# A Transformer block on one core: more buffers for keys, features and values, feature sums taken whole, and another written order

## The chip, the cores and the metric

The kernel runs on one core of a Trainium2 chip. A core has five engines with instruction queues of their own: TensorE (PE, matmuls), VectorE (DVE), ScalarE (ACT), GpSimd (POOL) and SyncE (SP, which here only issues DMAs). Every queue runs in order, and an instruction that depends on another engine waits for its semaphore. The metric is the device time of one execution in microseconds (us); lower is better.

## What is computed

For x of shape 2048 x 448 in bf16, the block is a linear attention with softmax feature maps, followed by a gated MLP, both on a layer-normalized input and both added back:

```python
def _A_ref(x, wqkv, w_phi, wo):                      # 16 heads of 28
    qkv = (x @ wqkv).reshape(B, S, 3, H, Dh) ...     # q, k, v
    pq = jnp.einsum("bhsd,hdf->bhsf", q, w_phi); pk = jnp.einsum("bhsd,hdf->bhsf", k, w_phi)
    phi_q = concat([softmax(pq), softmax(-pq)]); phi_k = concat([softmax(pk), softmax(-pk)])
    kv = jnp.einsum("bhsf,bhsd->bhfd", phi_k, v); z = jnp.einsum("bhsf->bhf", phi_k)
    num = jnp.einsum("bhqf,bhfd->bhqd", phi_q, kv)
    den = jnp.einsum("bhqf,bhf->bhq", phi_q, z)[..., None] + 1e-6
    return (num / den) ... @ wo
def _B_ref(x, w_gate, w_up, w_down):                 # F = 1792
    return (sigmoid(x @ w_gate) * (x @ w_up)) @ w_down
h = x + _A_ref(_layernorm(x), ...); h2 = h + _B_ref(_layernorm(h), ...)
```

## The kernel before

The 2048 rows are 16 tiles of 128 rows, numbered t; two neighbouring tiles are a pair, pr. All weights and all of x stay in SBUF.

**Start.** x and the weights are loaded. The feature weights are folded into the key and query weights on TensorE (kT, WkT, wM, W2: lines 535 to 575), so that keys come out of one matmul as feature logits. 14 matmuls on a zero tile (fill, line 988) run while the weights load.

**K/V stage, tile by tile.** bst and agg (lines 583, 585) are the layernorm's statistics on VectorE; ve and rstd (586, 588) give the reciprocal deviation, the power on GpSimd; xn (602 on ScalarE, 603 on VectorE) normalizes a tile into one of NXP buffers. Tiles 0 to 3 are transposed on TensorE (xP, xT), the others two at a time by a DMA transpose that SyncE issues (xT, line 621). pa and pb (line 637) are the two halves of a tile's matmuls: seven pairs that run side by side in the two row halves of the array, one for the key logits, one for v. ScalarE takes exp(l) and exp(-l) into ek (ekp 657, ekm 659), one of NEK buffers. v is copied out of PSUM into v1 (one of NV buffers) on ScalarE or VectorE; the copy and most PSUM evictions have the helper's line 425.

Each of the 32 softmaxes of a row (16 heads, two signs) needs its sum over 28 features. In the kernel before, sa (line 667) adds the two halves of the 28 pairwise into an f32 tile half_s, on GpSimd (12 tiles) or VectorE (4 tiles), and ss (673, VectorE) reduces the rest. rs (682) is the reciprocal, and phi (684) multiplies ek by it, 896 elements per partition, into one of NPHI buffers: all 16 on VectorE. kv (696) accumulates phi-transpose times v over the tiles in one PSUM bank; after tile 15, kvz (751, VectorE) takes the sums out.

**Attention stage.** q (line 736) are eight groups of matmuls, (gp, c) for two head groups and four chunks of 512 rows, with exponentials eqp and eqm on ScalarE. They need no kvz and stand between the K/V matmuls as well. num (772) are the numerators of one tile, ocp takes them out of PSUM (ScalarE or VectorE, line 425); rSm, rr, b, c, rd and o (788 to 800, VectorE) combine and divide; pair 0 is transposed on TensorE (oP, oT), the others by DMA (od, oT); wo (833) is the output projection; bst2, agg2, ve2, rstd2, hn (867 to 877) normalize h again; hP/hT transpose it.

**MLP.** Chunks of 2, 4, 4, 4 and 2 tiles. ga and gu (line 934) are the gate and up matmuls of one of 14 slices; sig (943, ScalarE) takes a tanh, hh (951, VectorE) multiplies; dn (968) is the down projection, fin (975) adds it to x, st (978) stores. The attention of the later pairs runs between the gate and up matmuls.

**The order is written out.** Every piece of work is a task with a name, an engine, a cost that only a planner uses, and the tasks that it depends on. With the text ORDER non-empty, no planner runs: `stored` (line 129) reads the order of all tasks from it, and `emit` (250) gives each task to its engine's queue in that order, with the waits that the dependencies need:

```python
for v in table.split():
    t = self.tasks[names[int(v) // 32]]
    t.eng = t.engs[int(v) % 4]
    ...
        t.got, gate = t.banks[int(v) // 4 % 8]
```

So each number holds the task (in order of creation, times 32), the PSUM banks (times 4) and which of the task's possible engines runs it.

Of the kernel before, what the change touches and what calls it, by code (L numbers as in the profile page):

```python
# [5 lines left out]
dt = mybir.dt  # L6
ALU = mybir.AluOpType
# [3 lines left out]
P = 128  # L11
D = 448
# [20 lines left out]
NFILL = 14  # L33
# [288 lines left out]
def build(nc, A_x, A_wqkv, A_w_phi, A_wo, B_w_gate, B_w_up, B_w_down, out):  # L322
# [13 lines left out]
    out_t = out[0].rearrange("(n p) d -> p n d", p=P)  # L336
    wd_v = B_w_down.rearrange("(ft p) n -> p ft n", p=P)

    NXP, NEK, NPHI, NV, NOP, NO, NHP, NSG, NSA = 8, 4, 3, 4, 3, 2, 2, 4, 2
    SPLIT = range(NT)  # L340

    with ExitStack() as es:
# [686 lines left out]
```

## Time and profile before

| | |
|---|---|
| time, median of 3 runs | 208.22 us (207.96 to 210.22) |
| the profiled execution | 207.67 us, of which its span is 205.9 us |
| TensorE busy | 197.2 us (96%) |
| VectorE busy | 135.6 us (66%) |
| ScalarE busy | 96.5 us (47%) |
| GpSimd busy | 30.6 us (15%) |
| granted TensorE clock | 1.00 |

The span runs from the first to the last instruction that the profiler recorded. Shares are averages over stages with different limits, so a stage has to be read by itself. A row of the lists of groups names the line, the engine, the operation, what it writes and reads with the shape, the count, the busy time with the mean duration in ns, and the idle time before it with what ended it. A timeline row has the start, the time from the first to the last end of the merged instructions, and the idle time in brackets. Two instructions in a row on VectorE overlap a little at their ends, so the spacing of their starts is shorter than their duration.

### The profile page before, as it was taken

Reading aid. Unit: us, or ns where it says so; the run is one execution under the profiler, and the core shown is the slowest. Engines: PE = TensorE matmul, PEld = TensorE weight load, DVE = VectorE, ACT = ScalarE, POOL = GpSimd, SP = SyncE. Lnnn points to the kernel's source line nnn. Section 1 sums busy time; section 2 is a strip of 40 time slices with the busy share of each in tenths; the row PEclk is TensorE's granted clock in tenths of the full one; section 3 lists DMA queues with packets and bytes.
Section 4 is the critical chain, followed back from the end, with each engine's and each line's share of the span. In section 5 each row is a group of like instructions: output and inputs, shape, how many; then the busy total and the mean of one; then the engine's idle time right before and its main releaser. Section 6 shows DMA issues by size and latency. Waiting matters only on the chain.

```text
span 205.9 us, 5431 instructions
## 1 busy us (share of the span) xinstructions
PE 197.2 (96%) x2278; PEld 107.1 (52%) x2278; DVE 135.6 (66%) x312; ACT 96.5 (47%) x172; POOL 30.6 (15%) x56
## 2 busy tenths in 40 slices
PE   7899998998988999999999999999999999999993
PEld 2544555455445876554444444544444455796553
DVE  2999999997998996789823875435446415351241
ACT  2579999799998773443311333003334400442000
POOL 3738653420003110001100001100001000000000
PEclk9999999999999999999999999999999999999999
DMA  5996477764022493700450000620000031000034
GB/s 167 279 277 128 76 188 200 181 223 142 3 57 48 73 173 81 197 3 3 94 111 3 0 0 3 124 51 0 3 0 5 2 79 20 0 3 0 25 111 156
DMA packets 35109, 16.94 MB, mean 82 GB/s; under 512 B 26828, under 2 KB 34060, under 8 KB 35084
## 3 DMA queue, kind: packets, MB, share of 16 engines
q1 hardware_dynamic: 34140, 15.78, 33.1%
q10 hardware_dynamic: 944, 0.80, 1.4%
q8 instruction: 18, 0.29, 0.6%
q14 instruction: 7, 0.06, 0.1%
HBM read 8.98 MB, written 1.84 MB: 53 GB/s over the span
## 4 chain that ended last, share of the span: by engine, by line
PE 78%; DVE 12%; ACT 4%; DMA 2%; issue 1%; POOL 1%
PE bank L934 42%; PE bank L968 21%; PE bank L637 5%; PE bank L833 4%; PE bank L736 3%; DMA x_sb<-in_A_x_dram 2%; DVE phi L684 2%; PE bank L696 1%; DVE ssum L673 1%; DVE xn_pad L603 1%; DVE st L583 1%; ACT xn_pad L602 1%; ACT ek L659 1%; DVE b_sb L792 1%; DVE b_sb L795 1%
## 5 line engine op out<-in xcount | busy, mean ns | idle before, releaser
L934 PE MATMUL bank<-xnT,wg_sb 64*128 64x512 bf16 (+1 forms) x490 | 87.4, 333 | 0.1
L934 PE MATMUL bank<-xnT,wu_sb 64*128 64x512 bf16 (+1 forms) x490 | 87.4, 333 | 0.0
L943 ACT ACTIVATE sg_sb<-bank 128x512 f32<-128x512 f32 (+1 forms) x70 | 34.6, 513 | 77.9 <-PE bank L934 74.0
L951 DVE SCALAR_TENSOR_TENSOR hh<-sg_sb,bank 128x512 bf16<-128x512 f32 (+1 forms) x70 | 39.1, 576 | 28.4 <-ACT sg_sb L943 28.1
L934 PEld LDWEIGHTS bank<-xnT,wg_sb 64*128 64x128 bf16 x490 | 45.3, 94 | 21.9 <-issue 1.9
L934 PEld LDWEIGHTS bank<-xnT,wu_sb 64*128 64x128 bf16 x490 | 45.1, 94 | 15.5
L968 PE MATMUL bank<-wd_sb,hh 128*128 128x448 bf16 (+1 forms) x238 | 43.1, 342 | 0.0
L968 PEld LDWEIGHTS bank<-wd_sb,hh 128*128 128x128 bf16 x238 | 22.9, 98 | 20.1 <-issue 1.4
L975 DVE SCALAR_TENSOR_TENSOR x_sb<-bank,x_sb 128x448 bf16<-128x448 f32 (+1 forms) x17 | 9.9, 594 | 28.3 <-PE bank L968 28.3
L637 PE MATMUL bank<-Wk,xnT 64*128 64x448 bf16 x112 | 22.1, 350 | 0.4 <-ACT Wq L425 0.3
L637 PE MATMUL bank<-Wv,xnT 64*128 64x448 bf16 x112 | 21.6, 350 | 0.0
L746 ACT ACTIVATE eq<-bank 128x1024 bf16<-128x1024 f32 x16 | 16.3, 1067 | 0.7 <-PE bank L736 0.6
L871 POOL TENSOR_SCALAR rs<-mv 128x2 f32<-128x2 f32 x5 | 1.3, 256 | 99.6 <-DVE mv L869 50.3
L667 POOL TENSOR_TENSOR half_s<-ek 128x448 f32<-128x448 bf16 x12 | 12.9, 1078 | 15.3 <-ACT ek L657 7.0
L425 ACT CAST opm<-bank 128x960 bf16<-128x960 f32 x14 | 13.7, 1014 | 2.8 <-PE bank L772 2.1
L833 PE MATMUL bank<-wo_sb,oT 64*128 64x448 bf16 x112 | 13.3, 350 | 0.9 <-DVE oT L425 0.6
L736 PE MATMUL bank<-xnT,Wq 64*128 64x512 bf16 x112 | 14.0, 377 | 0.1
L637 PEld LDWEIGHTS bank<-Wk,xnT 64*128 64x128 bf16 x112 | 9.1, 94 | 6.9 <-PE bank L637 1.0
L637 PEld LDWEIGHTS bank<-Wv,xnT 64*128 64x128 bf16 x112 | 9.2, 94 | 4.3
L684 DVE TENSOR_TENSOR phi<-ek,rsum 128x896 bf16<-128x896 bf16 x16 | 10.3, 655 | 0.3 <-PE bank L696 0.2
L583 DVE BATCH_NORM_STATS2 st<-x_sb 128x6 f32<-128x448 bf16 x16 | 9.4, 612 | 1.7 <-DMA x_sb<-in_A_x_dram 1.7
L657 ACT ACTIVATE ek<-bank 128x448 bf16<-128x448 f32 x16 | 9.7, 630 | 1.3 <-PE bank L637 1.3
(91 smaller groups left out, 185.4 us busy)
## 6 DMA issues: line engine op xcount, KB each, us to landing
wg_sb<-in_B_w_gate_dram SPq DMA_DIRECT2D x4, 448.0 KB, 3.8
wu_sb<-in_B_w_up_dram SPq DMA_DIRECT2D x4, 448.0 KB, 3.7
out_dram<-x_sb SPq DMA_DIRECT2D x15, 112.0 KB, 1.8
wd_sb<-in_B_w_down_dram SPq DMA_DIRECT2D x7, 224.0 KB, 2.7
x_sb<-in_A_x_dram SPq DMA_DIRECT2D x2, 448.0 KB, 5.8
wq_raw<-in_A_wqkv_dram SPq DMA_DIRECT2D x4, 128.0 KB, 5.3
x_sb<-in_A_x_dram SPq DMA_DIRECT2D x2, 224.0 KB, 4.5
x_sb<-in_A_x_dram ACTq DMA_DIRECT2D x2, 224.0 KB, 4.9
```

The source lines that it names most:

```text
L425: return e.copy(dst, src) if hasattr(e, "activation") else e.tensor_copy(dst, src)
L583: task(("bst", t), "dve", dve(D), lambda e, t=t: e.bn_stats(st1[:, t % 4, :], X(t)), [x_ld[t], opt(("agg", t - 4))])
L637: r = e.matmul(bank[bk][:, 0:D], lhsT=half(xnT, hi)[:, t, k, :], rhs=half(w, hi)[:, k, :], start=(i == 0), stop=(i == 6), tile_position=(6 ...
L667: task(("sa", t), None, 0.88, lambda e, t=t, s=s: e.tensor_tensor(half_s[:, t % NSA].rearrange("p (a n) -> p a n", a=4 * G), ek[:, s].rear ...
L684: task(("phi", t), None, 1.68, lambda e, t=t, s=s: e.tensor_tensor(phi[:, t % NPHI, :, :, 0:DH, :].rearrange("p a g d h -> p (a g) d h"), ...
L736: r = e.matmul(bank[bb[j]], lhsT=half(Wq2, hi)[:, k, 2 * g:2 * g + 2].rearrange("p c d h -> p (c d h)"), rhs=half(xnT, hi)[:, 4 * c:4 * c ...
L746: task((key, gp, c), "act", act_p(1024), lambda e, gp=gp, c=c, sg=sg, nm=nm: e.activation(eq[c][:, sg, 2 * gp:2 * gp + 2, :], wide[got(nm) ...
L833: r = e.matmul(bank[bb[j]][:, 0:D], lhsT=half(oT, hi)[:, pr % NO, j, k, :], rhs=half(wo_sb, hi)[:, k, :], start=(i == 0 and not res), stop ...
L934: r = e.matmul(bank[b][:, 0:N], lhsT=half(w, hi)[:, k, fs], rhs=half(hnT, hi)[:, t0:t0 + n, k, :], start=(i == 0), stop=(i == 6), tile_pos ...
L943: task(("sig", f_, c), "act", act_p(N), lambda e, j=j, N=N, nm=nm: e.activation(sg_sb[:, j % NSG, 0:N], bank[got(nm)[0]][:, 0:N], ACT.Tanh ...
L951: task(("hh", f_, c), "dve", dve(N), lambda e, j=j, N=N, nm=nm, f_=f_, c=c: e.scalar_tensor_tensor(hhT[c % 2][:, f_, 0:N], sg_sb[:, j % NS ...
L968: r = e.matmul(bank[b][:, c0:c1], lhsT=hhT[c % 2][:, f_, o:o + P], rhs=wd_sb[:, f_, c0:c1], start=(f_ == 0), stop=(f_ == FT - 1))
```

## The change

Five things change. (1) The buffers of xn go from 8 to 10, ek from 4 to 6, phi from 3 to 6, v1 from 4 to 6, and opm (what ocp writes) from 3 to 4 pairs. (2) SPLIT is empty: the 16 sa tasks and half_s go, and ss reduces all 28 features of each softmax from ek. (3) Ten of the 16 phi run on GpSimd: tiles 0, 1, 2, 4, 6, 7, 10, 11, 12 and 14. (4) 12 fill matmuls stand in place of 14. (5) ORDER is another table. Two dependencies are stated more exactly (which transposes free an xn or an o_pad buffer), and xn asks for its engine by the task, not by the engine object.

```diff
-NFILL = 14
+NFILL = 12
...
-    NXP, NEK, NPHI, NV, NOP, NO, NHP, NSG, NSA = 8, 4, 3, 4, 3, 2, 2, 4, 2
-    SPLIT = range(NT)
+    NXP, NEK, NPHI, NV, NOP, NO, NHP, NSG, NSA = 10, 6, 6, 6, 4, 2, 2, 4, 2
+    SPLIT = ()
...
-        half_s = sb("half_s", [P, NSA, D], dt.float32)
+        half_s = sb("half_s", [P, NSA, D], dt.float32) if len(SPLIT) else None
...
-                free = opt(("xT", (t - NXP) // 2 * 2)) or opt(("xT", t - NXP))
+                free = opt(("xT", t - NXP if t - NXP in PE_X else (t - NXP) // 2 * 2))
...
-                    if hasattr(e, "activation"):
+                    if K.tasks[("xn", t)].eng == "act":
...
-                fac(rden[:, s2], DH), ALU.mult), [("rd", pr), opt(("oT", pr - NO))])
+                fac(rden[:, s2], DH), ALU.mult), [("rd", pr), opt(("oT", pr - NO)), opt(("oT", pr - NO, 0)), opt(("oT", pr - NO, 1))])
```

The form of ss that then runs was in the kernel already, for tiles not in SPLIT:

```python
task(("ss", t), "dve", dve(896), lambda e, s=s: e.tensor_reduce(
    ssum[:, s, :].rearrange("p (a h) -> p a h", h=2),
    ek[:, s].rearrange("p a (g d h) -> p (a g) h d", g=2 * G, h=2), AX.X, ALU.add),
```

Read out of the two tables, the queues around the change are these (name and tile; one line break has no meaning).

VectorE before, from the first statistics to kvz:

```
bst0 agg0 ve0 bst1 agg1 xn0 bst3 bst2 agg3 agg2 xn1 bst7 bst6 xT1 bst5 xn2 xn3 xT0 bst4 agg5 agg6 agg4 agg7 ve4
bst9 bst10 bst8 nm4 xn4 xn5 agg9 agg10 agg8 bst11 agg11 ss0 rs0 v1.0 ve8 phi0 ss1 bst13 bst15 xn8 bst14 rs1 agg15
agg13 bst12 ss2 phi1 rs2 ss3 agg14 agg12 rs3 ve12 phi2 phi3 mm12 v1.5 ss4 ss5 rs4 rs5 phi4 sa6 phi5 xn13 ss6 rs6
ss7 rs7 phi6 phi7 ss8 rs8 phi8 xn14 v1.10 ss9 sa10 ss10 rs9 rs10 phi9 sa12 ss11 phi10 ss12 rs11 phi11 rs12 ss13
phi12 rs13 sa15 phi13 ss15 rs15 ss14 phi15 rs14 phi14 kvz
```

VectorE after:

```
bst0 bst1 agg0 agg1 ve0 ve1 bst3 agg3 bst2 xn0 xn1 bst5 agg2 bst4 ve2 bst6 agg5 bst7 agg6 agg4 agg7 xn2 ve4 xn3 mm4
xT2 nm4 xn4 xn5 bst10 xn6 bst8 bst9 bst11 agg10 agg8 agg11 agg9 ss1 ss0 rs0 xn9 rs1 bst14 bst15 bst13 ss2 agg13 rs2
bst12 ss3 agg12 agg14 agg15 xn10 rs3 ss4 ss5 xn13 rs4 xn12 ss7 rs7 rs5 phi3 phi5 xn14 xn15 ss6 ss8 rs6 rs8 ss9 ss11
phi8 rs9 rs11 ss10 ss12 rs10 phi9 v1.13 rs12 ss13 ss14 rs13 rs14 phi13 ss15 rs15 phi15 kvz
```

VectorE behind kvz, to the first normalized h: before `ocp1 ocp3 rSm0 rr0 b0 rSm1 c0 rr1 b1 rd0 c1 o0 rd1 rSm2 o1 rr2 od1 oT0 oT0 b2 c2 rd2 o2 od2 bst2 ... b3 c3 hn1 hn0`, after `ocp0 rSm0 rr0 ocp3 b0 rSm1 c0 rSm2 rr1 rr2 rd0 b1 o0 c1 rSm3 rd1 b2 oT0 o1 od1 c2 rd2 rr3 o2 b3 od2 bst2.0 bst2.1 agg2 agg2 hc0 ve2 ocp8 hn1 hn0`.

GpSimd after: `... rstd8 nm8 phi0 phi1 phi2 ve12 mm12 rstd12 nm12 phi4 phi7 phi6 phi11 phi10 phi12 phi14`, then the later reciprocal deviations.

TensorE after, from the first V matmuls: `va0 wM wM vb0 xP2 xP3 pa0 pb0 pa3 pb3 pa2 pb2 wM wM wM pa5 pa4 pb5 pa6 pb4 pb6 pa7 wM kv0 kv1 pb7 qa0.0 kv2 q0.0 pa9 pa8 pb9 pb8 pa11 kv3 kv4 kv5 pb11 pa10 pa12 pb10 qa1.0 pb12 q1.0 kv6 kv7 kv8 pa13 pa14 pb13 pb14 pa15 qa1.1 pb15 q1.1 qa0.1 kv9 q0.1 kv10 kv11 kv12 kv13 kv14 kv15 qa0.3 num0 ...`.

SyncE's loads: before `x0 wk1 wph x4 wq0 wq3 x8 wq2 wv0 wv1 wq1 x12` with wk0, x2 and x6 on ScalarE's queue; after `x0 wk1 wk0 x4 wph x6 wv1 wv0 wo wq3 wq2 wq1 wq0 x8 x12` with x2 alone on ScalarE's.

93 rows, old and new, of the table ORDER are left out of this document.

## The prediction

> **What bounds the kernel now.** I read the busy time by stretches first, cutting the span at TensorE's first K/V matmul (11.76 us), at the first read of the feature sums (49.38) and at the first gate/up matmul (66.45). Columns: busy us of each engine with its instructions, clock, DMA.
>
> ```profile
> core 0: us, PE busy (x) PEld busy (x) DVE busy (x) ACT busy (x) POOL busy (x), PEclk, DMA share, GB/s
> 0.00:11.76 11.76, 9.74 (x66) 4.99 (x66) 7.58 (x21) 5.29 (x10) 5.76 (x22) 1.00 0.92 236
> 11.76:49.38 37.62, 36.64 (x568) 18.81 (x567) 35.51 (x87) 34.67 (x66) 17.36 (x21) 1.00 0.73 181
> 49.38:66.45 17.07, 14.65 (x300) 7.92 (x299) 15.75 (x38) 16.18 (x21) 1.62 (x2) 1.00 0.17 33
> 66.45:205.90 139.45, 136.19 (x1354) 75.32 (x1350) 76.73 (x168) 40.38 (x78) 5.82 (x11) 1.00 0.22 49
> ```
>
> In the last stretch TensorE idles 3.26 us, nearly all of it behind its last matmul. The MLP is matmul after matmul, and nothing in the change touches its work: whatever is won or lost is the time of the first gate/up matmul. In the K/V stretch TensorE idles only 0.98 us and in the next 2.42, so a better order can save about 3.4 us there. But VectorE is busy 35.51 of 37.62, and it ends the chain at both seams. The chain of waits (start, us, what), then VectorE's and TensorE's timelines (start, us; idle time before and who ended it in brackets):
>
> ```profile
> 42.90 0.86 PE bank L736 x8
> ...
> 48.64 0.75 PE bank L736 x6
> 49.39 0.41 PE bank L772 x16
> ...
> 63.75 0.42 DVE hn_pad L877
> 64.17 0.05 issue
> 64.22 0.72 PE bank L887 x8
> 64.94 0.86 PE bank L833 x8
> ...
> 202.75 0.39 DVE x_sb L975
> ```
>
> ```profile
> 7.79 1.03 DVE L603 TENSOR_SCALAR xn_pad<-x_sb,mv,rs 128x512 bf16<-128x512 bf16 x1
> ...
> 16.03 0.62 DVE L673 TENSOR_REDUCE ssum<-half_s 128x32 f32<-128x448 f32 x1
> ...
> 47.18 0.62 DVE L684 TENSOR_TENSOR phi<-ek,rsum 128x896 bf16<-128x896 bf16 x1
> 48.68 0.64 DVE L751 TENSOR_TENSOR kvz<-bank,dmask 128x464 bf16<-128x464 f32 x1 [0.88 <-PE bank L696]
> ...
> 55.41 0.61 DVE L800 TENSOR_TENSOR o_pad<-b_sb,rden 128x896 bf16<-128x896 bf16 x1
> ...
> 63.75 0.73 DVE L877 TENSOR_SCALAR hn_pad<-x_sb,mv,rs 128x512 bf16<-128x512 bf16 x2 [0.60 <-POOL rs L873]
> ```
>
> These are my anchors: first feature sum 16.03, last scaling done 47.80, kvz 48.68, first attention output 55.41, first normalized h 63.75.
>
> **The change, part by part.** The unit prices (groups by line and form: busy, mean ns) and the spacing of two operations in a row (timeline):
>
> ```profile
> L667 POOL TENSOR_TENSOR half_s<-ek 128x448 f32<-128x448 bf16 x12 | 12.9, 1078 | 15.3 <-ACT ek L657 7.0 <-ACT ek L659 3.7 <-DVE ssum L673 3.6
> L524 POOL TENSOR_TENSOR Wp<-wphd,maskW 112x224 bf16<-112x224 bf16 x2 | 1.1, 559 | 0.0
> L863 DVE TENSOR_TENSOR x_sb<-bank,x_sb 128x896 bf16<-128x896 f32 x7 | 7.6, 1086 | 0.4 <-PE bank L833 0.3
> L425 DVE CAST opm<-bank 128x960 bf16<-128x960 f32 x2 | 2.2, 1152 | 0.5 <-PE bank L772 0.5
> L425 DVE CAST v<-bank 128x448 bf16<-128x448 f32 x3 | 1.8, 603 | 0.3 <-PE bank L696 0.3
> L873 POOL TENSOR_TENSOR rs<-rs,neghalf 128x2 f32<-128x2 f32 x8 | 6.2, 770 | 5.8 <-DVE rs L871 5.4
> ```
>
> ```profile
> 6.51 1.15 DVE L583 BATCH_NORM_STATS2 st<-x_sb 128x6 f32<-128x448 bf16 x2
> 10.65 0.71 DVE L603 TENSOR_SCALAR xn_pad<-x_sb,mv,rs 128x512 bf16<-128x512 bf16 x2
> 23.67 1.15 DVE L684 TENSOR_TENSOR phi<-ek,rsum 128x896 bf16<-128x896 bf16 x2
> 25.74 1.14 DVE L673 TENSOR_REDUCE ssum<-half_s 128x32 f32<-128x448 f32 x2
> 26.80 0.55 DVE L682 RECIPROCAL rsum<-ssum 128x32 bf16<-128x32 f32 x2
> ```
>
> Two half sums take 1.14 us where one takes about 0.61, so the spacing is 0.53; likewise 0.53 for a scaling (phi), 0.54 for a bn_stats, 0.33 for a normalization (xn), 0.27 for a reciprocal (rs).
>
> *Full sums.* A reduction over 896 elements is not in the trace. The two casts from PSUM differ by 549 ns for 512 elements, 1.07 ns each; 448 more elements on top of 0.53 make a step of 1.00 us. The 896-element add of L863 took 1.086, the upper end; 0.53 would be the lower end, if the bf16 input were read twice as fast as the f32 one. I take 1.00, nearest to L863, which also has 896 elements. Sixteen add 16 x 0.47 = 7.5 us to VectorE.
>
> *Pairwise adds* go: four on VectorE (4 x 0.53 = 2.1), twelve on GpSimd (12.9 us).
>
> *Ten scalings to GpSimd.* VectorE loses 10 x 0.53 = 5.3. On GpSimd the two rows give 0.56 us for 224 elements and, undisturbed, 0.97 for 448 (row at 19.89 below: two in 1.90): by the line through both 1.79 for 896, by doubling 1.94. I take 1.8, since overhead doesn't double. GpSimd gets 18 us for 12.9, still far from full, but one scaling is 1.3 us slower than on VectorE.
>
> *Moved by the order:* four normalizations to VectorE (+1.3), two v evictions (about -1.1) and one xT copy (-0.3) off it, by the tables that follow from the order (section on the change). VectorE's sum for the stretch changes by 7.5 - 2.1 - 5.3 + 1.3 - 1.4 = 0.0 us. So the move buys no VectorE time; what counts is the waits. The normalizations leave ScalarE, which had slack of 3 us; that cover costs nothing. Two fewer fill matmuls lie in the start, before the weights have landed: nothing.
>
> *Loads.* Tiles 8 to 11 of x move from seventh place in SyncE's queue to twelfth, behind Wv, one wo piece and the wq pieces; the twelfth was tiles 12 to 15 (DMA queue's timeline, then the page's issues):
>
> ```profile
> 4.20 0.52 SPq L461 DMA_DIRECT2D x_sb<-in_A_x_dram  x1
> ...
> 8.54 0.56 SPq L461 DMA_DIRECT2D x_sb<-in_A_x_dram  x1
> ```
>
> ```profile
> x_sb<-in_A_x_dram SPq DMA_DIRECT2D x2, 448.0 KB, 5.8
> ```
>
> Issued near 8.5 with 5.8 to landing they are there by 14.3; their first bn_stats stands at about 14.2 in the sum below, so at most 0.1 shows, and without that cover each later us would delay VectorE's whole stretch. wk0 goes from ScalarE's queue to third on SyncE's, x6 to sixth; Wv comes earlier, which lets the first V matmuls start before K's. I cost these at nothing.
>
> *Waits.* VectorE and GpSimd exclude each other where both read SBUF in these forms:
>
> ```profile
> 28.81 1.06 DVE L603 TENSOR_SCALAR xn_pad<-x_sb,mv,rs 128x512 bf16<-128x512 bf16 x1
> 31.57 1.87 DVE L684 TENSOR_TENSOR phi<-ek,rsum 128x896 bf16<-128x896 bf16 x2
> ```
>
> ```profile
> 19.89 1.90 POOL L667 TENSOR_TENSOR half_s<-ek 128x448 f32<-128x448 bf16 x2 [0.44 <-ACT ek L657]
> 28.49 1.23 POOL L667 TENSOR_TENSOR half_s<-ek 128x448 f32<-128x448 bf16 x1 [1.52 <-ACT ek L657]
> 31.79 1.16 POOL L667 TENSOR_TENSOR half_s<-ek 128x448 f32<-128x448 bf16 x1 [0.28 <-ACT ek L659]
> ```
>
> The normalization at 28.81 took 1.06 instead of 0.41 and ended 0.15 us behind GpSimd's add (29.72). At 31.57 two scalings took 1.87 instead of 1.15: GpSimd's add, asked for in the first, ran between them. So a blocked operation waits for the whole of the other, and the one already waiting goes next. The Trainium skill, "SBUF — State Buffer", section "Who interferes with whom", says this too: a VectorE instruction with two SBUF inputs contends with a GpSimd instruction that reads SBUF, and the second to issue fully blocks. It speaks against this change, since the blocker grows from 0.97 to 1.8 us; these rows agree. Without it the waits below would be nil (first rival).
>
> Now VectorE's new queue, added up. xn1 ends at about 8.7, as before (8.82). Six batches of statistics and two normalizations bring it to 12.4; xT2 waits for tile 2's transposes, which stand behind the first V matmuls on TensorE, until 13.0; then xT2, nm4, xn4, xn5, xn6, four bn_stats and four aggregations: the first sum starts at **17.15, 1.1 later** than 16.03. From there to phi15: 16 sums 16.0, 16 reciprocals 4.3, 6 scalings 3.2, 6 normalizations 2.0, 4 bn_stats and 4 aggregations 2.6, one v 0.5: 28.6 us. Before, the same count gives 28.9 of 31.8, so 2.9 were waits. New waits, from placing GpSimd's scalings behind their reciprocals: xn10 behind phi2 0.25; phi3 behind phi4 0.25; phi5 behind phi7 1.8 (phi7 waited while phi3 ran, so it goes first); phi13 behind phi12 0.35; phi15 behind phi14 0.45: 3.1. phi15 ends at 17.15 + 28.6 + 3.1 = **48.85, against 47.80**.
>
> The six buffers let TensorE run on to tile 7 about 2 us earlier, but kv3 to kv5 stand in its queue ahead of tile 11's matmuls and wait for phi3 (31.0) and phi5 (33.3), some 3 us in which nothing else behind them can run. By kvz TensorE has four q groups done, not five: the lead is gone. kvz comes 0.6 after phi15: 49.4 (+0.7). TensorE then finishes a q half (0.86) before num0. ocp0 1.2, rSm0 and rr0 0.5, ocp3 1.15, b0 0.55 and eight more small ones 2.6: o0 ends at 56.5, against 56.0 (+0.5). Behind it c1 to b2 1.8, oT 0.35, o1 to od2 2.85, two bn_stats with their aggregations 1.35, hc0 (now on VectorE) and ve2 0.65: 63.5. GpSimd's power takes 0.8, but ocp8 (1.15) stands before hn1: hn1 at **64.7, +0.95**. From hn1 to the first gate/up matmul the kernel before takes 2.7 us (63.75 to 66.45: transposes, the third output projection, one num); the new order has a second num there (0.25): 67.65 (+1.2), and that num is then done, so nothing more is late than **+0.95 us** at the end.
>
> The profiled execution took 207.67 us (span 205.9 and 1.8 around it), so 208.6 by this sum; the median of the runs, 208.22, lies 0.55 above the profiled time, so **209.2** for the median.
>
> **Rivals.**
> - *The waits don't come* (faster, 0.22). If GpSimd's scalings fall between VectorE's, the 3.1 us go; TensorE then bounds the stretch and about 2.1 reach the end: 207.1. For it: reductions and reciprocals, two thirds of VectorE's time, never waited in the rows above. Against: six VectorE scalings and six normalizations stand beside ten GpSimd operations of 1.8.
> - *GpSimd keeps the pair* (slower, 0.20). If its next scaling, already queued, goes ahead of a waiting VectorE one, phi13 waits for phi12 and phi14: +1.35; with 1.94 per scaling another 0.6 in four waits: 211.2. It decides where two GpSimd scalings are ready in a row (phi4 and phi7, phi12 and phi14). For it: 28.49 to 31.79 shows one handover each way only.
> - *Buffers hide it* (the change does nothing, 0.13): kvz stays, one num less: 208.0.
> - *The reduction reads bf16 faster* (0.06): 7.5 us off VectorE, of which TensorE's idle time allows 3: 205.2.
>
> **How the numbers follow.** The forecast (208.2 to 210.3: the sum, and a microsecond of error in placing GpSimd's scalings to either side) has 0.39, the rivals 0.22, 0.20, 0.13 and 0.06 as given. About 1%, 2.1 us, is what a measurement of this kernel can tell from no change. Faster by more than that needs the last rival or the upper part of the first: 0.18. Slower: the second rival and the forecast's upper tail, 0.26. Same 0.56. A range of 206.0 to 211.9 leaves out the last rival, a part of the first and the tail of the second, together under 0.2; sums at L863's 1.086 would add 1.4 and stay in it.
>
> **What would show it.** Sums of about 1.06 us each, GpSimd scalings of 1.8, VectorE scalings above 1 us beside them, TensorE idle before kv3 and kv5 (L696) by 3 us, kvz at 49.4, hn at 64.7, first gate/up at 67.65. The forecast is wrong if kvz comes before 48.5, or if the normalized h comes no later than 63.75 in spite of a late kvz.

## The result and the profile after

| | before | after |
|---|---|---|
| median of the runs, us | 207.68 (207.17 to 210.22, 20 runs) | 206.62 (205.79 to 208.32, 20 runs) |
| the profiled execution, us | 207.67, span 205.9 | 205.79, span 204.0 |
| first feature sum starts | 16.03 | 15.95 |
| last scaling done | 47.80 | 45.86 |
| kvz starts | 48.68 | 46.81 |
| first normalized h | 63.75 | 61.89 |
| first gate/up matmul | 66.45 | 65.02 |

The ratio is 0.995, with a 95% interval of 0.9933 to 0.9967: 1.1 us, or 0.5%, faster. The forecast was 209.2, slower by a microsecond. The time lies in its range and on the other side of no change. The profiled execution happens to be the fastest of its twenty runs, 0.83 us below their median, so the differences between the two profiles are larger than that between the medians. Two further profiles of the changed kernel have spans of 204.4 and 205.1.

The busy time of the K/V stretch, cut at the same times as in the prediction:

```profile
core 0: us, PE busy (x) PEld busy (x) DVE busy (x) ACT busy (x) POOL busy (x), PEclk, DMA share, GB/s
...
11.76:49.38 37.62, 36.15 (x620) 19.18 (x619) 35.14 (x69) 34.87 (x66) 20.90 (x19) 1.00 0.80 179
```

VectorE is as busy as before (35.14 against 35.51), in 69 instructions instead of 87; GpSimd has 3.5 us more. TensorE has 620 matmuls there instead of 568, but kvz now comes at 46.81 and the window reaches 2.6 us into the attention stage with its short matmuls: by busy time TensorE does not do more there (36.15 against 36.64).

The two new kinds of work, in the page's groups by line (count, then busy us, mean ns, idle time before):

```profile
L683 POOL TENSOR_TENSOR phi<-ek,rsum 128x896 bf16<-128x896 bf16 x10 | 17.8, 1784 | 8.0 <-DVE rsum L681 7.4
L677 DVE TENSOR_REDUCE ssum<-ek 128x32 f32<-128x896 bf16 x16 | 16.5, 1064 | 0.4 <-ACT ek L656 0.4
```

VectorE's timeline of the changed kernel, and then GpSimd's:

```profile
6.95 0.72 DVE L602 TENSOR_SCALAR xn_pad<-x_sb,mv,rs 128x512 bf16<-128x512 bf16 x2
...
12.04 0.42 DVE L424 COPY xnT<-bank 128x512 bf16<-128x512 bf16 x1 [1.05 <-PE bank L612]
...
15.95 2.04 DVE L677 TENSOR_REDUCE ssum<-ek 128x32 f32<-128x896 bf16 x2
...
27.16 1.09 DVE L677 TENSOR_REDUCE ssum<-ek 128x32 f32<-128x896 bf16 x1 [0.39 <-ACT ek L656]
...
28.77 2.58 DVE L683 TENSOR_TENSOR phi<-ek,rsum 128x896 bf16<-128x896 bf16 x2
...
43.26 0.56 DVE L683 TENSOR_TENSOR phi<-ek,rsum 128x896 bf16<-128x896 bf16 x1
43.74 1.07 DVE L677 TENSOR_REDUCE ssum<-ek 128x32 f32<-128x896 bf16 x1
...
45.24 0.62 DVE L683 TENSOR_TENSOR phi<-ek,rsum 128x896 bf16<-128x896 bf16 x1
46.81 0.64 DVE L750 TENSOR_TENSOR kvz<-bank,dmask 128x464 bf16<-128x464 f32 x1 [0.95 <-PE bank L695]
```

```profile
7.44 1.16 POOL L523 TENSOR_TENSOR Wp<-wphd,maskW 112x224 bf16<-112x224 bf16 x2 [0.63 <-DMA wphd<-in_A_w_phi_dram]
...
26.62 1.70 POOL L683 TENSOR_TENSOR phi<-ek,rsum 128x896 bf16<-128x896 bf16 x1 [1.28 <-DVE rsum L681]
28.72 2.15 POOL L683 TENSOR_TENSOR phi<-ek,rsum 128x896 bf16<-128x896 bf16 x1 [0.41 <-DVE rsum L681]
...
39.66 3.58 POOL L683 TENSOR_TENSOR phi<-ek,rsum 128x896 bf16<-128x896 bf16 x2 [0.51 <-ACT eq L745]
43.43 1.94 POOL L683 TENSOR_TENSOR phi<-ek,rsum 128x896 bf16<-128x896 bf16 x1 [0.18 <-DVE rsum L681]
```

From the first sum to the end of the last scaling VectorE takes 29.9 us (15.95 to 45.86) where it took 31.8 (16.03 to 47.80). In this piece it is blocked once for long. Of the two VectorE scalings merged in the row at 28.77, phi3 took 0.56 us and phi5 2.11 (the minimum and the maximum in the view of the tile phi). GpSimd's scaling at 28.72 (phi7) takes 2.15 us, 0.45 more than the one before it and about the time of phi3, and phi5 then waits for the rest of it. At 43.26 VectorE's scaling begins 0.02 us behind the end of GpSimd's two (39.66 + 3.58).

TensorE says more. The same busy table, cut at its first K or V matmul and at kvz, first of the kernel before, then of the changed one:

```profile
11.76:48.68 36.92, 35.94 (x564) 18.71 (x564) 34.87 (x86) 34.00 (x65) 17.36 (x21) 1.00 0.74 181
```

```profile
9.57:46.81 37.24, 35.92 (x571) 18.96 (x572) 34.67 (x75) 34.81 (x67) 22.08 (x20) 1.00 0.84 185
```

Cut so, TensorE begins 2.19 us earlier, with V matmuls, has the same 35.9 us of work and 0.34 us more idle time, and kvz comes 1.87 earlier. But the two stretches do not hold the same work: folds and transposes that came ahead of the first K matmul are in it now, and eight q matmuls are not. TensorE's first fold of the query weights (wM0, out of WqT) is a better cut, since both kernels have the same matmuls ahead of it, two fills aside. Its row in TensorE's timeline and the busy table from there to kvz, before and then after:

```profile
17.81 0.90 PE L555 MATMUL bank<-Wp,WqT 112*128 112x112 bf16 x12
```

```profile
17.55 0.76 PE L554 MATMUL bank<-Wp,WqT 112*128 112x112 bf16 x12 [0.51 <-DMA WqT<-wq_raw]
```

```profile
17.81:48.68 30.87, 30.02 (x508) 16.30 (x508) 28.95 (x65) 28.88 (x55) 13.83 (x16) 1.00 0.66 173
```

```profile
17.55:46.81 29.26, 28.66 (x498) 15.86 (x500) 27.78 (x53) 26.94 (x51) 19.52 (x16) 1.00 0.76 171
```

At the fold 0.26 us of the early start are left. The rest went into the folds and transposes that now stand between (7.26 us of work from the first K or V matmul to the fold instead of 5.92) and into idle time, 0.51 us of it waiting for the transposed query weights (WqT). In the two further profiles the fold starts at 18.15 and 18.43, later than before. The gain comes behind the fold: kvz follows it by 29.26 us instead of 30.87, with 1.36 less work and 0.25 less idle time. The eight q matmuls are 0.7 of that work (8.03 and 7.32 us on their line); the rest is on lines with the same matmuls before and after, and what shortened them was not taken apart.

The chain of waits of the changed kernel through the same stretch (start, us, what):

```profile
11.88 5.62 DMA WqT<-wq_raw
...
17.55 0.76 PE bank L554 x12
18.31 2.26 PE bank L636 x21
...
20.59 0.53 ACT v L424
...
26.70 0.45 ACT ek L656
...
27.16 1.10 DVE ssum L677
...
28.85 2.51 DVE phi L683 x2
...
31.41 0.44 PE bank L695 x16
31.84 2.75 PE bank L636 x28
...
45.13 1.64 PE bank L695 x96
```

It runs through four bounds in turn: the landing of the transposed query weights (WqT), TensorE, an unbroken ScalarE list from 20.59 to 27.14, VectorE for 4 us with the blocked pair in it, and from 31.41 TensorE alone. Before, VectorE stood in this chain until 35.0, and TensorE alone followed from there (in the kernel before):

```profile
34.39 0.64 DVE phi L684
...
35.07 0.44 PE bank L696 x16
```

From kvz to the first gate/up matmul the kernel takes 18.2 us instead of 17.8 (65.02 - 46.81, 66.45 - 48.68), and from there to the end 139.0 instead of 139.5: the eight q matmuls and one more num are done ahead of the first gate/up matmul, and the two nearly cancel. So 1.87 at kvz comes out as 1.9 of span. In the two further profiles kvz comes at 47.38 and 47.68, so only 1.3 and 1.0 us earlier than before.

### The profile page after: what moved, and what is told of

It is laid out like the page before. It is cut to its first block, busy times and chain, and to the rows that moved or that the text cites. A ratio compares the mean times of both kernels' runs of the same rounds, so it can differ in the third digit from the quotient of the medians.

```text
span 204.0 us, 5395 instructions
## 1 busy us (share of the span) xinstructions
PE 196.3 (96%) x2276; PEld 109.2 (54%) x2276; DVE 135.3 (66%) x304; ACT 94.7 (46%) x169; POOL 34.5 (17%) x51
## 4 chain that ended last, share of the span: by engine, by line
PE 81%; DVE 6%; DMA 5%; ACT 4%; SPq 3%; issue 1%; DVEq 0%
PE bank L933 42%; PE bank L967 21%; PE bank L636 5%; PE bank L832 5%; PE bank L735 4%; DMA WqT<-wq_raw 3%; SPq L460 3%; DMA wq_raw<-in_A_wqkv_dram 2%; PE bank L695 2%; DVE phi L683 1%; PE bank L771 1%; ACT v L424 1%; ACT ek L656 1%; ACT ek L658 1%; SPq L500 1%
## 5 line engine op out<-in xcount | busy, mean ns | idle before, releaser
L683 POOL TENSOR_TENSOR phi<-ek,rsum 128x896 bf16<-128x896 bf16 x10 | 17.8, 1784 | 8.0 <-DVE rsum L681 7.4
L677 DVE TENSOR_REDUCE ssum<-ek 128x32 f32<-128x896 bf16 x16 | 16.5, 1064 | 0.4 <-ACT ek L656 0.4
L872 POOL TENSOR_TENSOR rs<-rs,neghalf 128x2 f32<-128x2 f32 x8 | 5.6, 697 | 60.0 <-DVE rs L870 59.8
L424 ACT CAST opm<-bank 128x960 bf16<-128x960 f32 x13 | 12.1, 976 | 1.4 <-PE bank L771 1.4
L862 DVE TENSOR_TENSOR x_sb<-bank,x_sb 128x896 bf16<-128x896 f32 x7 | 7.5, 1085 | 3.4 <-PE bank L832 3.4
L658 ACT ACTIVATE ek<-bank 128x448 bf16<-128x448 f32 x16 | 8.8, 558 | 1.2 <-PE bank L636 1.1
```

The costliest lines, as they stand in the source:

```text
L424: return e.copy(dst, src) if hasattr(e, "activation") else e.tensor_copy(dst, src)
L658: task(("ekm", t), "act", act_p(D), lambda e, t=t, s=s: e.activation(ek[:, s, 1, :], bank[got(k_at[t][0])[k_at[t][1]]][:, 0:D], ACT.Exp, s ...
L677: task(("ss", t), "dve", dve(896), lambda e, s=s: e.tensor_reduce(ssum[:, s, :].rearrange("p (a h) -> p a h", h=2), ek[:, s].rearrange("p ...
L683: task(("phi", t), None, 1.68, lambda e, t=t, s=s: e.tensor_tensor(phi[:, t % NPHI, :, :, 0:DH, :].rearrange("p a g d h -> p (a g) d h"), ...
```

## The experiments

Ratios are to the kernel before, run on the same chip; 0.001 is 0.2 us. "After" has 0.995 by its twenty runs, and 0.9965 and 0.9956 where it was measured again (below), so a difference to it is uncertain by some 0.3 us. A profile is one execution, up to 1.2 us from the median of its runs. An order is told by the queues that it gives.

**Parts of the change, in the order of before.** First the buffers alone (opm stays at 3, since half_s takes the room of a fourth), then also the full sums, all 16 scalings on VectorE, then also ten scalings on GpSimd:

```diff
-    NXP, NEK, NPHI, NV, NOP, NO, NHP, NSG, NSA = 8, 4, 3, 4, 3, 2, 2, 4, 2
+    NXP, NEK, NPHI, NV, NOP, NO, NHP, NSG, NSA = 10, 6, 6, 6, 3, 2, 2, 4, 2     # first
+    SPLIT = ()          and NOP 4, the sa tasks out of the order     # second
+    GpSimd: phi0 phi1 phi2 phi4 phi6 phi7 phi10 phi11 phi12 phi14     # third
```

> The kernel before with its own order and work, and the larger buffers of xn, ek, phi and v1 (10, 6, 6, 6; opm stays at 3, since with half_s there is no room for a fourth). Theory ScalarE: the gain of 1.06 us (207.68 to 206.62) comes from ScalarE's shorter list in the K/V stretch, so buffers alone give 0.0 us, ratio 1.000. Theory VectorE: GpSimd's scalings cost VectorE fewer waits than forecast, and that is the gain; buffers alone 0.0 us. Theory buffers: TensorE runs further ahead; about -1.0 us, ratio 0.995.

> The kernel before's order with the larger buffers and the full sums on VectorE (no pairwise adds); all scalings on VectorE. VectorE's list gets 16 x 0.44 = 7.0 us more and 2.1 less, GpSimd loses its 12.9 us of adds. Theory balance (VectorE and ScalarE bound the K/V stretch together, a microsecond on either costs 0.5 to 1): +2.5 to +4.5 us, ratio 1.012 to 1.022. Theory VectorE alone: +4.9 us, ratio 1.024.

> The same with the ten scalings on GpSimd as well, still in the kernel before's order: 5.3 us off VectorE again, 18 us on GpSimd, and the seven normalizations that ScalarE had before stay there. Theory balance: VectorE's work is that of the kernel before, ScalarE's too, and this order wasn't searched with the lock, so the waits of VectorE for GpSimd grow by 1 to 2 us; +0.5 to +2.0 us, ratio 1.003 to 1.010. If the scalings on GpSimd by themselves were the gain: ratio 0.995.

The buffers alone: 206.95 us, 0.9989 (0.9981 to 0.9998), 0.2 us faster. With the full sums: 209.69 us, 1.0118 (1.0105 to 1.0131), 2.4 us slower, the low end of what was expected. VectorE is then the bound: the row of the stretch from the first K/V matmul to kvz has it busy for 38.12 of 39.32 us, with 2.8 us of idle time on TensorE.

```profile
11.54:50.86 39.32, 36.51 (x564) 18.97 (x564) 38.12 (x82) 34.84 (x66) 4.81 (x9) 1.00 0.60 160
```

With the ten scalings on GpSimd as well: 210.51 us, 1.0158 (1.0145 to 1.0171). This missed. It takes work off the engine that is the bound and is slower still. Its table of waits between 12 and 52 us (engine and line, waited for; us in total, times, longest):

```profile
PEld bank L695 <- POOL phi L683: 3.7, 6, 1.0
...
PE bank L695 <- POOL phi L683: 2.3, 4, 0.9
```

TensorE's matmuls of kv stand where they stood, and a scaling takes 1.7 us on GpSimd for 0.56. They wait 2.3 us for GpSimd's scalings, its weight loads 3.7. In the kernel with the full sums alone the same view has 2.3 and 3.3 us of waits for VectorE's scalings: taking ten of them off VectorE has not shortened TensorE's waits, only given them another cause. Where the additional 0.8 us come from this does not show. So neither the buffers nor the full sums nor the ten scalings make the kernel faster by more than 0.2 us in the order of before (the four normalizations were not moved in it); only with another order do they.

**Parts of the order taken back.** From the changed kernel: the normalizations of tiles 9, 10, 12 and 15 back on ScalarE; or all 16 scalings back on VectorE.

```diff
 ScalarE
-... ekp2 v12 W20.3 ... W20.0 v14 ... eqp0.0 eqm0.0 ... ekp8 ekm9 ...
+... ekp2 v12 xn9 W20.3 ... W20.0 xn10 v14 ... eqp0.0 xn12 eqm0.0 ... ekp8 xn15 ekm9 ...
```

```diff
 VectorE
-... xn9 rs1 bst14 bst15 bst13 ss2 ... rs12 ss13 ss14 rs13 rs14 phi13 ss15 rs15 phi15 kvz
+... xn9 rs1 phi0 bst14 bst15 bst13 phi1 ss2 ... phi10 rs12 ss13 phi12 ss14 ... ss15 phi14 rs15 phi15 kvz
```

> The changed kernel with the normalizations of tiles 9, 10, 12 and 15 on ScalarE again, as before; all else as changed. ScalarE gets 4 x 0.7 = 2.8 us more, VectorE 1.3 us less. Theory ScalarE: its rows run back to back from 11.7 to 29.1 us, so the feature sums come later; +1.0 to +2.0 us against the changed kernel, ratio to the kernel before 1.000 to 1.005. Theory VectorE: its list bounds the stretch and gets shorter; -0.5 to -1.0 us, ratio 0.990 to 0.993.

> The changed kernel with all 16 scalings on VectorE, at the same places of the order. VectorE gets 10 x 0.53 = 5.3 us more and loses the waits of 1.5 us for GpSimd. Theory VectorE: +3.5 us against the changed kernel, ratio to the kernel before 1.012. Theory ScalarE: VectorE has a microsecond or two to spare while ScalarE bounds, so +1.5 to +2.5 us, ratio 1.002 to 1.007.

The first: 207.18 us, 0.9996 (0.9984 to 1.0007), so 0.6 to 1 us of the gain is gone with four normalizations of 0.7 us. VectorE, 1.3 us lighter, waits for ScalarE's exponentials instead (the longest of these waits, in its timeline):

```profile
28.92 1.08 DVE L677 TENSOR_REDUCE ssum<-ek 128x32 f32<-128x896 bf16 x1 [1.58 <-ACT ek L656]
```

The second: 208.74 us, 1.0072 (1.006 to 1.0084), 2.2 to 2.5 us slower than the changed kernel; VectorE's timeline shows no wait between 12.2 and kvz at 49.54. So the GpSimd scalings are worth over 2 us in an order that has room for them.

**One list made longer.** Which engine's list sets the time? In each of four kernels one list of the changed kernel gets about 1.8 us of additional work, written to a tile that nobody reads at that time (the result is unchanged): the full sums of two tiles computed twice (VectorE), or both exponentials of two tiles twice (ScalarE); early is tiles 1 and 3, late tiles 11 and 13.

```diff
+TWICE = (1, 3)          # late: (11, 13)
-  e.tensor_reduce(ssum[:, s], ek[:, s], ...)
+  [e.tensor_reduce(o, ek[:, s], ...) for o in ([ssx[:, TWICE.index(t)]] if t in TWICE else []) + [ssum[:, s]]][-1]
   # ScalarE: the same for the exponentials ekp and ekm
```

> The changed kernel with the feature sums of tiles 1 and 3 taken twice on VectorE (the first time into a scratch tile): 2 x 0.97 = 1.9 us more, between 16 and 24 us. Theory two limits: ScalarE bounds the stretch up to about 27 us and VectorE after it, and VectorE's list has only the 0.4 us that it waits for the exponentials of tile 7 at 27.16; so +1.5 us against the changed kernel, ratio to the kernel before 1.002. Theory ScalarE alone: VectorE has room before 27 us; +0.0 to +0.5 us, ratio 0.994 to 0.997.

> The same with the sums of tiles 11 and 13: 1.9 us more on VectorE, between 33 and 44 us. Theory two limits: +1.9 us against the changed kernel, ratio 1.004. Theory ScalarE alone: +0.0 to +0.5 us, ratio 0.994 to 0.997.

> The changed kernel with both exponentials of the keys of tiles 1 and 3 taken twice on ScalarE (the first time into a scratch tile): 4 x 0.42 = 1.7 us more, between 14 and 18 us. Theory two limits and theory ScalarE alone: ScalarE works back to back there, so the exponentials behind come 1.7 us later and +1.3 to +1.7 us reach the end, ratio 1.001 to 1.003. Theory VectorE alone: VectorE's list bounds, with 0.4 us or less; +0.3 us, ratio 0.996.

> The same with the exponentials of tiles 11 and 13: 1.7 us more on ScalarE, between 30 and 39 us, where it waits for TensorE five times (0.2 to 0.7 us each). Theory two limits: hidden by those waits, 0.0 to +0.5 us, ratio 0.995 to 0.997. Theory ScalarE alone: +1.5 us, ratio 1.002.

| | us | ratio | over after, us |
|---|---|---|---|
| VectorE early | 208.25 | 1.0041 (1.0017 to 1.0065) | 1.9 |
| VectorE late | 207.64 | 1.0007 (0.9988 to 1.0025) | 1.2 |
| ScalarE early | 207.55 | 0.9989 (0.9961 to 1.0016) | 0.8 |
| ScalarE late | 207.47 | 0.9998 (0.9979 to 1.0017) | 1.0 |

No list is the only bound. By the medians a microsecond costs 0.5 to 1 us wherever it is put, late in ScalarE's list too, where 0 to 0.5 was expected; VectorE late and ScalarE early cost less than the 1.9 and 1.3 to 1.7 us expected. The intervals reach some 0.5 us to either side, so the four places are not told apart. The work reappears as a wait of the next engine in the ring: TensorE for VectorE's scaling with VectorE's list longer (first row, TensorE's timeline, VectorE early; 0.60 in the changed kernel), VectorE for ScalarE's exponentials with ScalarE's (second row, VectorE's timeline, ScalarE late):

```profile
32.84 0.44 PE L698 MATMUL bank<-v,phi 128*64 128x58 bf16 x16 [1.33 <-DVE phi L686]
```

```profile
43.00 2.08 DVE L680 TENSOR_REDUCE ssum<-ek 128x32 f32<-128x896 bf16 x2 [1.00 <-ACT ek L660]
```

**The lock's wait taken away.** GpSimd's phi7 needs rs7. If VectorE's phi3 and phi5 stand ahead of rs7, phi7 cannot be asked for while they run. Or phi5 goes to GpSimd as well.

```diff
 VectorE
-... xn12 ss7 rs7 rs5 phi3 phi5 xn14 xn15 ss6 ss8 rs6 rs8 ...
+... xn12 ss7 rs5 phi3 phi5 rs7 ss6 ss8 xn14 xn15 rs6 rs8 ...     # first
+... xn12 ss7 rs7 phi3 xn14 xn15 rs5 ss6 ss8 rs6 rs8 ss9 ss11 rs9 rs11 phi8 ...   # second; GpSimd: phi4 phi5 phi7
 SyncE
-... xT12 xT14 wg1 wg2 ...
+... xT12 wg1 xT14 wg2 ...                # first
```

> The changed kernel with VectorE's scalings of tiles 3 and 5 ahead of the reciprocal of tile 7, which GpSimd's scaling of tile 7 needs, and the sums of tiles 6 and 8 ahead of the normalizations of tiles 14 and 15. So the scaling of tile 5 no longer meets GpSimd's of tile 7 (the pair took 2.58 us in place of 1.15). Theory VectorE: the 1.4 us come off the stretch and about -1.0 us reach the end, ratio to the kernel before 0.990. Theory ScalarE: 0.0 to -0.3 us, ratio 0.994 to 0.995.

> The changed kernel with the scaling of tile 5 on GpSimd too, between those of tiles 4 and 7, the normalizations of tiles 14 and 15 moved ahead of the reciprocal of tile 5, and the scaling of tile 8 behind the reciprocals of tiles 9 and 11. VectorE loses 0.5 us of work and the 1.4 us that the scalings of tiles 3 and 5 waited. Theory balance: -1.0 to -1.5 us against the changed kernel, ratio to the kernel before 0.988 to 0.990. Theory ScalarE alone: 0.0, ratio 0.995.

The first: 205.94 us, 0.9928 (0.9903 to 0.9952), with runs from 204.72 to 208.13. The pair takes 1.09 us instead of 2.58 (VectorE's timeline), and the chain of waits no longer leaves TensorE between WqT's landing and kvz:

```profile
28.84 1.09 DVE L683 TENSOR_TENSOR phi<-ek,rsum 128x896 bf16<-128x896 bf16 x2
```

```profile
11.81 6.11 DMA WqT<-wq_raw
...
17.97 0.76 PE bank L554 x12
18.73 4.88 PE bank L636 x50
...
44.79 1.64 PE bank L695 x96
```

A second measurement of it, beside the changed kernel on one chip:

> The changed kernel, on the same chip as the next: ratio to the kernel before 0.995 to 0.9965.

> The changed kernel without VectorE's wait of 1.4 us at the scalings of tiles 3 and 5, and so without TensorE's wait of 0.8 us at kv5. If the lock's waits count: -0.5 to -0.9 us against the changed kernel on this chip, ratio 0.991 to 0.993. If ScalarE hides them: within 0.2 us of it.

The changed kernel 206.73 us, 0.9956 (0.994 to 0.9972); the order without the wait 205.55 us, 0.9909 (0.9889 to 0.9929): the edit that removes the 1.5 us of blocking is worth 1.0 (by the ratios) to 1.2 us (by the medians) there. In both profiles of this order TensorE has no idle time from the query fold to kvz, 28.49 us of work. The edit also moves two sums and a weight load (see the queues); their share was not taken apart.

The second edit missed: 206.76 us, 0.9964 (0.9945 to 0.9983), beside 206.52 us, 0.9965 (0.9952 to 0.9977), of the changed kernel on that chip:

> The changed kernel once more, as the anchor on this chip: ratio to the kernel before 0.995, as first measured (0.9933 to 0.9967).

No VectorE scaling is blocked, but phi5 comes later from GpSimd, kv5 waits for it on TensorE, and with TensorE's keys late VectorE waits for exponentials (TensorE's timeline, then VectorE's):

```profile
32.58 0.44 PE L695 MATMUL bank<-v,phi 128*64 128x58 bf16 x16 [1.03 <-POOL phi L683]
```

```profile
35.19 1.09 DVE L677 TENSOR_REDUCE ssum<-ek 128x32 f32<-128x896 bf16 x1 [1.02 <-ACT ek L658]
```

**The landing of WqT.** If TensorE's list is the bound from there on, that landing should set the time. Two pairs of edits moved it, one of them the wrong way. The first put the transposes of tiles 4 and 6 ahead of WqT's on SyncE and the query fold later on TensorE (with its evictions on ScalarE), so that TensorE need not wait for it; the second of the pair has the order without the blocked pair as well.

```diff
 SyncE
-... x8 x12 wqT1 wqT0 xT4 xT6 ...
+... x8 x12 xT4 xT6 wqT1 wqT0 ...
 TensorE
-... pa2 pb2 wM0.1 wM0.3 wM0.2 pa5 pa4 pb5 pa6 pb4 pb6 pa7 wM0.0 kv0 ...
+... pa2 pb2 pa5 pa4 pb5 wM0.1 pa6 pb4 wM0.3 pb6 wM0.2 pa7 wM0.0 kv0 ...
```

> The changed kernel with SyncE's transposes of tiles 4 to 7 ahead of those of the query weights, and the fold of the query weights (four groups on TensorE, with their evictions on ScalarE) spread behind the key matmuls of tiles 4 to 7 instead of ahead of them. TensorE no longer waits 0.7 to 1.5 us at 16.7 us. Theory TensorE's queue: that wait reaches the end in part, -0.5 to -1.0 us against the changed kernel, ratio to the kernel before 0.990 to 0.994. Theory ScalarE: its rows have no gap there in the profile of the changed kernel, so 0.0 to -0.2 us, ratio 0.995 to 0.9965; the profile would then show ScalarE back to back and TensorE waiting for evicted banks instead.

> The same with VectorE's scalings of tiles 3 and 5 ahead of the reciprocal of tile 7 as well, which takes away the wait at kv5. Theory TensorE's queue: another -0.5 us, ratio 0.987 to 0.991. Theory ScalarE: the second part alone, ratio 0.993 to 0.995.

Both missed: 209.6 us, 1.0113 (1.0096 to 1.013), and 210.53 us, 1.0148 (1.0128 to 1.0168). WqT landed at 21.8 instead of 17.5; the fold in its new place was still too early, TensorE waited for WqT and ScalarE for the fold's result, with exponentials behind it (TensorE's timeline, then ScalarE's):

```profile
21.82 0.37 PE L554 MATMUL bank<-Wp,WqT 112*128 112x112 bf16 x4 [1.59 <-DMA WqT<-wq_raw]
```

```profile
22.22 0.53 ACT L424 CAST Wq<-bank 128x448 bf16<-128x448 f32 x1 [3.56 <-PE bank L554]
```

kvz came at 50.41, 3.6 later than in the changed kernel, as much as this hole in ScalarE's list; by the ratios the edit costs 3.1 to 3.4 us. Why the second kernel of the pair is slower still was not followed up.

The second pair brings the landing forward. The early load of wo, 0.99 us on SyncE's queue and needed only in the attention stage, goes behind xT6; in the changed kernel, and in the order without the blocked pair.

```diff
 SyncE
-x0 wk1 wk0 x4 wph x6 wv1 wv0 wo wq3 wq2 wq1 wq0 x8 x12 wqT1 wqT0 xT4 xT6 ...
+x0 wk1 wk0 x4 wph x6 wv1 wv0 wq3 wq2 wq1 wq0 x8 x12 wqT1 wqT0 xT4 xT6 wo ...
```

> The changed kernel, with SyncE's one early load of wo (issued from 5.15 to 6.14 us there, needed only by the output projections from about 55 us) moved behind the two transposes xT4 and xT6. The query-weight loads and the transposes WqT behind them are then issued 0.99 us earlier. Theory that the landing of WqT sets the start of the stretch (17.55, 18.15 and 18.43 us in three profiles of the changed kernel, with spans of 204.0, 204.4 and 205.1, and TensorE idle 0.5 to 1.0 just before): TensorE's idle time before the query fold goes and the time falls by 0.3 to 0.9 us, ratio to the kernel before 0.991 to 0.994. Rival, that TensorE's wait there is made good later, since VectorE and ScalarE have their own full lists: ratio as without the edit, 0.995 to 0.9965.

> The same move of wo, on top of the order in which phi3 and phi5 come before rs7. There TensorE runs without a gap from WqT's landing to kvz, so by the theory that this landing sets the start the gain is the whole of the idle time, 0.97 to 1.03 us: ratio 0.986 to 0.989. Rival: as that order alone, 0.991 to 0.993.

205.84 us, 0.9929 (0.9916 to 0.9943), as the theory of the landing had it, though the interval touches that of the changed kernel; and 205.03 us, 0.9893 (0.9879 to 0.9906), just short of its 0.986 to 0.989 and outside the rival's range. TensorE's first query fold, in two further profiles of the changed kernel (spans 204.4 and 205.1), then with wo later:

```profile
18.15 0.76 PE L554 MATMUL bank<-Wp,WqT 112*128 112x112 bf16 x12 [1.03 <-DMA WqT<-wq_raw]
```

```profile
18.43 0.77 PE L554 MATMUL bank<-Wp,WqT 112*128 112x112 bf16 x12 [0.98 <-DMA WqT<-wq_raw]
```

```profile
17.06 0.76 PE L554 MATMUL bank<-Wp,WqT 112*128 112x112 bf16 x12
```

The wait is gone. In the three profiles of the changed kernel kvz follows this fold by 29.26, 29.23 and 29.25 us: there the landing sets kvz one for one. With the other edit less than the whole of it is won, since the next transfer is then late: in the chain of waits of the last kernel stands the transpose of a normalized tile, landing at 18.15.

```profile
13.66 4.49 DMA xnT<-xn_pad
...
18.19 4.90 PE bank L636 x50
```

That last kernel, the changed one with two moves in its order, beats both: 1.1% faster than before, and its four runs lie between 205.00 and 205.31.

**All of them in one sum.** For twelve of the profiles, TensorE's first K or V matmul, its first query fold, its work and its idle time from that fold to kvz, in us (kvz is the sum of the last three):

| | first K/V | fold | work | idle | kvz |
|---|---|---|---|---|---|
| before | 11.76 | 17.81 | 30.02 | 0.85 | 48.68 |
| buffers alone | 11.65 | 17.70 | 29.85 | 0.28 | 47.83 |
| and full sums | 11.54 | 17.59 | 30.59 | 2.68 | 50.86 |
| and ten scalings on GpSimd | 11.47 | 17.52 | 31.11 | 2.85 | 51.48 |
| after | 9.57 | 17.55 | 28.66 | 0.60 | 46.81 |
| after, again | 9.66 | 18.15 | 28.63 | 0.60 | 47.38 |
| after, again | 9.99 | 18.43 | 28.65 | 0.60 | 47.68 |
| four normalizations on ScalarE | 9.99 | 18.62 | 29.02 | 0.94 | 48.58 |
| all scalings on VectorE | 9.71 | 17.69 | 29.29 | 2.56 | 49.54 |
| no blocked pair | 9.47 | 17.97 | 28.49 | 0.00 | 46.46 |
| wo later | 9.54 | 17.06 | 28.98 | 0.62 | 46.66 |
| no blocked pair, wo later | 9.89 | 17.30 | 28.61 | 0.12 | 46.03 |

The row behind one of them, no blocked pair:

```profile
17.97:46.46 28.49, 28.49 (x498) 15.94 (x500) 26.16 (x52) 26.42 (x49) 18.89 (x14) 1.00 0.76 175
```

From kvz to the end all of them take 157.0 to 157.4 us, so kvz tells the rest. The changed order lets TensorE start 1.5 to 2.3 us earlier, and at the query fold little or nothing is left of it: 17.55 to 18.62, with wo later 17.06 and 17.30, against 17.52 to 17.81. Behind the fold the full sums cost 2.4 us of idle time in the order of before. With the ten scalings on GpSimd and the order written for them it is 0.60, and with the scalings back on VectorE 2.56. The buffers alone show 0.6 us less idle time in their profile, of which their runs confirm 0.2 us. Which pieces of the order shorten TensorE's work from 29.9 to 28.7, beyond the eight q matmuls, no run here takes apart.

## Why the prediction was wrong

**The size of the miss and its place.** The sum gave 49.4 for kvz, 67.65 for the first gate/up matmul and 208.6 for the profiled execution; measured were 46.81, 65.02 and 205.79. The miss of 2.6 to 2.8 us stands complete at kvz.

**The step that failed: the sum of VectorE's queue, on which kvz was hung.** I added up that queue to phi15, 48.85, and put kvz 0.6 behind it. Measured was phi15's end at 45.86, with kvz 0.95 behind it, when TensorE was done. Of the 3.0 us of miss 1.2 are a first sum that I had too late, 1.6 are blocking that I counted and that did not come, and 0.6 are unit prices; 0.4 us of waits for exponentials, which I had not counted, go the other way. The next two points take them one by one.

**"VectorE ends the chain at both seams", and "the lead is gone".** VectorE left the chain of the kernel before at 35.0, and from there TensorE ran without a wait to kvz; its idle time in the stretch was 0.98 us, as I had quoted. I let TensorE wait 3 us at kv3 to kv5; it waited 0.6, in each of three profiles. So from the query fold to kvz TensorE is idle for 0.6 of 29.3 us and bounds the stretch. What sets the fold is the landing of WqT, which my sum does not have: TensorE waits 0.5 to 1.0 us for it. The early V matmuls, which I "cost at nothing", start TensorE 2.2 us earlier, and of these 0.26 or less are left at the fold. That price was about right.

**"The first sum starts at 17.15, 1.1 later."** It started at 15.95. I let xn1 end at about 8.7, as before, where its normalization took 1.03 us at 7.79 beside GpSimd's fold of Wp. In the new order both normalizations are done at 7.67, and Wp, waiting for its load until 7.44, is hardly in their way. Behind xn1 and ahead of xT2 the queue has four batches of statistics, not the six that I counted. VectorE was ready at 10.99 and waited for the transposes until 12.04, not 13.0: this wait decides, and makes 1.0 of the 1.2.

**The waits for GpSimd, "3.1".** The mechanism is as described: the alternation at 28.72, phi7 between phi3 and phi5, is the one that the prediction named, and it cost 1.5 us (2.58 against the 1.09 of the order without it) where 0.25 and 1.8 were summed. What I had as the first rival, whose waits don't come and whose TensorE then bounds the stretch (207.1), is nearest to the result. The time of 206.62 lies below the 208.2 to 210.3 of the sum itself; that it falls into the wider range of 206.0 to 211.9 is due to the part of this rival that the range takes in. The Trainium skill, "SBUF — State Buffer", section "Who interferes with whom", says that a reduction never contends with GpSimd on trn2; the trace agrees, as the sum at 43.74 takes 1.07 us inside GpSimd's scaling of 43.43 to 45.37, and 1.064 in the mean of all. But the other waits, 1.05 together at xn10, phi13 and phi15, all but vanished: phi13 found GpSimd's two scalings just done. I had placed GpSimd's scalings from a VectorE list that was itself more than a microsecond late. From the first sum on VectorE took 29.9 us and not 31.7: 1.6 less blocking, 0.4 more waiting for exponentials, and by difference 0.6 of unit prices that I had rounded up.

**"The normalizations leave ScalarE, which had slack of 3 us; that cover costs nothing."** This is the wrong reading of the profile, though in the sum it was a nothing and so moved no number. 34.67 busy of 37.62 is an average over the stretch. ScalarE's timeline of the kernel before shows no wait from its first exponential to 36.4:

```profile
13.54 0.54 ACT L659 ACTIVATE ek<-bank 128x448 bf16<-128x448 f32 x1 [0.93 <-PE bank L637]
...
37.74 0.54 ACT L657 ACTIVATE ek<-bank 128x448 bf16<-128x448 f32 x1 [1.34 <-PE bank L637]
```

All of its slack lies behind. In the changed kernel, too, ScalarE's list sets when the exponentials of the first half come, and four normalizations on it are worth 0.6 to 1 us, nearly the whole gain of the change: without that move it is 0.9996.

**Right**: VectorE's unchanged total (34.87 and 34.67 us from the first K/V matmul to kvz); 1.8 for a GpSimd scaling (1.784) and 1.00 for a step of the full sums (two in 2.04); that the lead that the buffers give does not reach the end (0.2 us for the buffers alone); that the changed order takes longer from kvz to the first gate/up matmul and has then done more (0.4 us longer, and 0.5 given back behind it, where 0.25 was foreseen); that the MLP gives and takes nothing else. The step from the profiled execution to the median went wrong by itself: I added 0.55, and it was 0.83.

**What stays open.** Why the landing of WqT varies between executions of the same kernel, from 17.5 to 18.4 us in three profiles, was not settled. In these three the transposes were issued at 11.88, 12.12 and 12.41 and took 5.6, 6.0 and 6.0 us; kvz follows the landing, and the spans are 204.0, 204.4 and 205.1 in the same order. That this is the whole spread of the changed kernel's runs is not shown. It fits the narrow spread with the load moved, 205.51 to 206.08, but those are six runs.

## What to carry to other kernels

In a stretch where one engine has hardly any idle time, add up that engine first: what it does and what it waits for. Compare two kernels from a point ahead of which both have done the same work; an earlier first matmul was no lead here, since work had been moved behind it and a load was waited for. Price the relief of another engine by whether its timeline has waits in the very piece where the work is taken away, not by its busy share: 92% busy was here 100% for 23 us and then holes. Where three engines with in-order queues feed each other and all are over 90% busy, a microsecond on any of them cost about half to the whole of it, and the longer latency of a slower engine (1.8 us for 0.56) paid only where the order was written for it.

## What the runs showed of the hardware

- VectorE and GpSimd, excluding each other, took turns: with one operation of each waiting, GpSimd's scaling ran between VectorE's two (28.72), in all three profiles of the changed kernel. The blocked pair took 2.58 us in each, the GpSimd scaling that waited 2.15 instead of 1.70.
- A scaling of 896 elements a partition takes 1.69 to 1.70 us on GpSimd undisturbed and 0.56 to 0.62 on VectorE.
- The transposing DMAs of the query weights, issued at the same place of SyncE's queue with the same loads ahead of them, landed 5.6 us after their issue in one profile (at 11.88, in the changed kernel), 6.0 in two others of the same kernel (at 12.12 and 12.41), and 6.1 in another (at 11.81, in the order without the blocked pair).
